# A linear-attention and expert kernel: the state's recurrence issued step by step, and the bonus of two units computed as a matrix product

## The chip, the cores and the metric

The kernel runs on one core of a Trainium2 chip (trn2). The time of a kernel is the device time in microseconds of one execution. A run of the profiler gives, for one execution, the start and the duration of each instruction on the engines: PE (TensorE, matrix products; PEld is its weight load), DVE (VectorE), ACT (ScalarE), POOL (GpSimd), and SP, which issues the DMAs. Engines run side by side, each through its own list of instructions in the order of the program; they wait for each other through semaphores.

## What is computed

The reference has two parts. The first is a recurrence over 768 tokens for 4 batches and 8 heads of width 48; the second is a set of 4 causal attention experts over its output, of which each token uses two.

```python
for t in range(S):                       # S = 768, D = 48
    cur = einsum('bhd,bhe->bhde', u * kt, vt)
    y[:, :, t] = einsum('bhd,bhde->bhe', rt, state + cur)
    state = wt[..., None] * state + einsum('bhd,bhe->bhde', kt, vt)
...
x = y.transpose(0, 2, 1, 3).reshape(B, S, H * D)
logits = x @ w_gate                      # the two largest of 4 experts, softmax over them
for e in range(E):                       # Hd = 64
    a = softmax(causal(x @ wq[e] @ (x @ wk[e]).T / 8))
    out += weight(e) * (a @ (x @ wv[e]) @ wo[e])
```

The term with `u` is called the bonus below: for a token it adds v, times the sum over d of r·u·k, to that token's own row and to no other.

## The kernel before

**Tiling.** The recurrence is cut into chunks of 64 tokens, so that a chunk's work is matrix products and only a 48 x 48 state per head goes from chunk to chunk. A unit is 384 tokens (6 chunks, 3 tiles of 128) of one batch; there are 8 units, and in each 4 pairs of heads. Names in the profile carry the unit and the pair: `ups4_20` belongs to unit 4, pair 2 (the last digit tells which of two banks). Units 0, 2, 4, 6 begin a batch, and 1, 3, 5, 7 go on with its state.

**One pair** (function `one`, L368 on). Two DMAs bring `lt` (decays w, then k, then r, with the head's dimension on the partitions: 391 + 384 + 384 columns) and `nat` (v, k and r, each 288 columns, with tokens on the partitions). DVE runs two scans over the decays, backwards into `suf` (L410) and, from the reciprocal of the chunk's product (L412), forwards into `pre` (L414). Then, on DVE or POOL as the planner decides: `kt` = k·suf (L417) and r·pre into `pre` (L419, called mr by the planner). The bonus is three operations: `nat`'s k times u (L423, uk), times r (L425, ur), and a sum over each head's 48 columns on DVE into `rk` (L428); ACT (L435) or DVE or POOL (L437) puts `rk` on the diagonal of `am` (dg). PE transposes `kt` (L447, then a copy to `kts`), makes the products inside a chunk (`aps`, L459), which DVE copies into `am` under a mask (L465), and the keys times values of each chunk (`ups`, L478, two banks of PSUM). The state's recurrence is L484: for each of the 6 chunks (5 in units 1, 3, 5 and 7, whose last state nobody needs) one DVE instruction of 112 x 48, new state = decay x old state + `ups`, each needing the one before. They are one entry of the plan, a function called `chain`, so they stand one behind the other. A state of each chunk, scaled by the decay (`ys`, L492), is what PE multiplies into `yb` (L513, for two pairs at once); `yi` (L526) is the chunk's own part from `am` and v. Their sum `xi` (L536) is split into a high and a low part, `xx` (L545 on ACT and L547; pair 3 goes to `xs` and from there through six small DMAs, L559, into the free rows of `xx`).

**One group** of the experts (function `moe`, L574 on) takes a unit's `xx`: projections of queries and keys (`pp`, L611), of values and gate logits (`vp`, L634), scores (`sp`, L702), a maximum on DVE (L708), the exponential on ACT (L714), transposes (`tp`, L727), the weighted values (`yp`, L758), the gates, and the output projection (`op`, L830). The last unit is two groups, 7 and 8.

**What sets the order.** Everything is recorded as entries with a cost per engine, and a planner (`Plan.order`, L128 on) puts them one after the other by due times, costs and the waits between engines that it assumes; the engine for an entry is chosen there too. Due times are shifted by tables of numbers per kind (`OFF`, `OFF0` for unit 0, `OFFE` per engine, `SH` per unit or group). What the planner leaves is the fixed list of each engine. Where it expects PE to wait for over a microsecond in the first 60, it adds matmuls without a use (L900), and 14 of them stand at the start (L874). PSUM's eight banks and the buffers of SBUF (`lt` has 3, for example) are planned in the same way: an entry cannot stand before its buffer is free. The chain is recorded so:

```python
plan.add("ss", {"DVE": 118 * nh}, chain, [suf, ku + (k % 2, 0)] + ups,
         [ku + (k % 2, 1)] + ([] if last else [ku + (1 - k % 2, 0)]))
```

Before anything else DVE builds masks (L290 to L319), and the weights of the experts are split into a high and a low part (L332 on ACT, L334 on DVE or POOL).

## Time and profile before

| what | us |
| --- | --- |
| median of 3 runs (lowest, highest) | 370.32 (367.99, 371.35) |
| the profiled execution, its own time | 371.82 |
| its span, first to last instruction | 370.0 |
| PE, DVE, ACT, POOL busy in the span | 335.5, 323.3, 223.8, 183.6 |

The mean clock that PE was granted is 0.962 of full speed. In lines of groups, `xcount | busy, mean ns | idle` is the number of instructions, their busy time in us with the mean duration of one in ns, and how long their engine stood idle before them, with what ended most of that. In a timeline the first column is the start in us and the second the time until the last of the merged instructions ends. A merged group's instructions overlap where the next one starts before the last has ended, so the starts tell the rate.

### The profile page before, as it was taken

What the parts mean: (1) busy time and instruction counts of PE and PEld (TensorE: products, weight loads), DVE (VectorE), ACT (ScalarE), POOL (GpSimd) and SP (SyncE); (2) the same over time, 40 slices, a digit from 0 to 9 for tenths busy, and PEclk for the clock granted to TensorE, in tenths of its full rate; (3) what the DMA queues carried; (4) which work ended last, traced back from release to release, by engine and by line L of the source; (5) the groups of instructions that cost most, each with busy time, mean ns of one, the idle gap of its engine ahead of it and who ended that gap; (6) DMA issues with size and microseconds to landing.
All of it is one profiled execution on the core that took longest, in us unless ns stands there. A gap on an engine that the chain in (4) does not pass through costs nothing.

```text
span 370.0 us, 12837 instructions
## 1 busy us (share of the span) xinstructions
PE 335.5 (91%) x5030; PEld 277.0 (75%) x5030; DVE 323.3 (87%) x989; ACT 223.8 (60%) x663; POOL 183.6 (50%) x311
## 2 busy tenths in 40 slices
PE   8847699689998998989899999889999999999996
PEld 3424469668887797889688697879787888898975
DVE  8997999879998899998999999998899988855871
ACT  2173344387576687474578692775587764854873
POOL 3524455464693383775556643773745743402120
PEclk9895999799997899999999999999999999999999
DMA  7835174252260355522322835352345201210101
GB/s 287 322 89 167 50 212 170 66 169 46 102 204 26 115 192 160 178 78 89 111 78 106 232 96 162 97 145 81 95 161 178 57 8 47 61 39 0 66 2 64
DMA packets 15470, 42.63 MB, mean 115 GB/s; under 512 B 2225, under 2 KB 6834, under 8 KB 15410
## 3 DMA queue, kind: packets, MB, share of 16 engines
q1 hardware_dynamic: 15410, 41.81, 35.8%
q8 instruction: 40, 0.66, 0.7%
q14 instruction: 20, 0.16, 0.2%
HBM read 34.73 MB, written 4.72 MB: 107 GB/s over the span
## 4 chain that ended last, share of the span: by engine, by line
PE 52%; DVE 35%; issue 5%; ACT 3%; DMA 3%; POOL 1%; SPq 0%; DVEq 0%; POOLq 0%; ACTq 0%
PE pp L611 10%; DVE ss L484 9%; PE tp L727 8%; PE op L830 6%; PE yp L758 6%; PE sp L702 6%; PE vp L634 5%; DVE pre L414 4%; DVE a L708 3%; DVE suf L410 3%; PE yi L526 3%; PE yb L513 2%; DVE xi L536 2%; DMA xx<-xs 2%; DVE pre L419 2%
## 5 line engine op out<-in xcount | busy, mean ns | idle before, releaser
L714 ACT ACTIVATE a<-a,mx 128x128 f32<-128x128 f32 (+5 forms) x96 | 63.8, 667 | 13.2 <-DVE mx L708 12.8
L435 ACT ACTIVATE am<-ident,rk 128x64 f32<-128x64 f32 x168 | 43.1, 337 | 23.4 <-DVE rk L428 23.4
L611 PE MATMUL pp<-xx,wh_qk 128*128 128x384 f32 (+2 forms) x216 | 56.5, 329 | 0.2 <-DMA xx<-xs 0.2
L727 PE MATMUL tp<-ident,a 128*128 128x128 f32 x336 | 48.1, 284 | 2.2 <-DVE ss L484 1.7
L484 DVE SCALAR_TENSOR_TENSOR ss<-ss,suf,ups 112x48 f32<-112x48 f32 x160 | 41.9, 263 | 7.8 <-PE ups L478 0.7
L708 DVE CUSTOM_DVE_ANT_0 a<-sp,cmask 128x384 f32<-128x384 f32 (+4 forms) x96 | 43.5, 496 | 2.3 <-PE sp L702 1.4
L419 POOL TENSOR_TENSOR pre<-lt,pre 128x384 f32<-128x384 f32 x24 | 23.7, 988 | 43.2 <-DVE pre L414 37.3
L727 PEld LDWEIGHTS tp<-ident,a 128*128 128x128 f32 x336 | 38.9, 145 | 6.8 <-ACT ATa L243 1.3
L611 PEld LDWEIGHTS pp<-xx,wh_qk 128*128 128x128 f32 x216 | 38.7, 188 | 1.3 <-DVE mx L708 0.5
L758 PE MATMUL yp<-ATa,v_sb 128*64 128x384 f32 (+2 forms) x256 | 36.5, 413 | 1.6 <-DVE ss L484 1.4
L423 POOL TENSOR_TENSOR nat<-nat,u_sb 128x288 f32<-128x288 f32 x28 | 27.8, 996 | 15.3 <-ACT u_sb L243 8.8
L611 PE MATMUL pp<-xx,wl_qk 128*128 128x384 f32 (+2 forms) x108 | 35.0, 324 | 0.0
L243 ACT COPY ATa<-tp 128x512 f32<-128x512 f32 (+3 forms) x69 | 30.6, 479 | 6.3 <-PE tp L727 5.9
L414 DVE TENSOR_TENSOR_SCAN pre<-lt,inv_pre 128x390 f32<-128x390 f32 x32 | 33.8, 1056 | 0.0
L417 POOL TENSOR_TENSOR kt<-lt,suf 128x384 f32<-128x384 f32 x28 | 29.7, 1062 | 8.1 <-DVE suf L410 4.9
L410 DVE TENSOR_TENSOR_SCAN suf<-lt,one_suf 128x390 f32<-128x390 f32 x32 | 32.7, 1033 | 0.5 <-DMA lt<-in_wkr_dram 0.5
L634 PE MATMUL vp<-wh_vg,xx 128*128 128x260 f32 x144 | 30.8, 294 | 0.4 <-DVE ss L484 0.2
L702 PE MATMUL sp<-Kh,Qh 64*128 64x384 f32 (+4 forms) x128 | 26.6, 368 | 4.2 <-DVE ss L484 4.2
L758 PEld LDWEIGHTS yp<-ATa,v_sb 128*64 128x64 f32 x256 | 18.1, 136 | 15.6 <-issue 8.0
L459 PE MATMUL aps<-pre,kt 64*64 64x64 f32 x768 | 20.0, 230 | 9.6 <-DVE am L465 3.5
L545 ACT CAST xx<-xi 112x384 fp32r<-112x384 f32 x24 | 12.2, 510 | 24.0 <-DVE xi L536 23.0
L459 PEld LDWEIGHTS aps<-pre,kt 64*64 64x64 f32 x768 | 16.2, 139 | 13.6 <-issue 5.8
(353 smaller groups left out, 862.4 us busy)
## 6 DMA issues: line engine op xcount, KB each, us to landing
lt<-in_wkr_dram SPq DMA_DIRECT2D x32, 579.5 KB, 4.8
nat<-in_nat_dram SPq DMA_DIRECT2D x32, 432.0 KB, 3.9
...
uf<-in_uN_dram SPq DMA_DIRECT2D x1, 1.5 KB
```

The costliest lines, as they stand in the source:

```text
L410: plan.add("suf", {"DVE": t_scan(wb)}, lambda e: nc.vector.tensor_tensor_scan(rev(suf(), wb), rev(w_(), wb), rev(one_suf, wb), 0.0, op0=AL ...
L414: plan.add("pre", {"DVE": t_scan(wb)}, lambda e: nc.vector.tensor_tensor_scan(pre()[:, 0:wb - 1], w_()[:, 0:wb - 1], flat(inv_pre[:, 0:nh] ...
L435: nc.scalar.mul(am()[:, h, i], ident2, rk()[:, i, h:h + 1])
L459: nc.tensor.matmul(aps[h]()[half(q), i * C:(i + 1) * C], kt()[half(h), c, :], pv()[half(h), c, 0:C], start=True, stop=True)
L484: nc.vector.scalar_tensor_tensor(sv(c + 1), zero[0:112] if c == s0 == 0 else sv(c), sfv()[0:112, c, 0:1], ups[c % 2]()[0:112, c // 2 * D:( ...
L611: nc.tensor.matmul(pp()[:, 0:W], w[:, qk, k, cs], xx()[:, x, k, x0:x0 + W], start=(k == j == 0), stop=(k == j == 2))
L634: nc.tensor.matmul(vp()[:, 0:260], xx()[:, x, k, o], w[:, k, :], start=(k == j == 0), stop=(k == j == 2))
L702: nc.tensor.matmul(sps[x]()[:, 0:w], q()[p, t], k()[p, o], start=j == 0, stop=j == 2)
L708: plan.add("max", {"DVE": t_dve(w) + T_RED}, lambda e, x=x, a=a, mx=mx, h=h, o=o, m=m, sps=sps: nc.vector.tensor_tensor_reduce(a()[:, o], ...
L714: plan.add("exp", {"ACT": t_exp(n)}, lambda e, x=x, y=y, mx=mx, a=a: nc.scalar.activation(a()[:, 0:n], a()[:, 0:n], AF.Exp, bias=mx[-1](), ...
L727: nc.tensor.transpose(tp()[:, j * 128:(j + 1) * 128], a()[:, (j0 + j) * 128:(j0 + j + 1) * 128], ident)
L758: nc.tensor.matmul(yp()[e * 64:e * 64 + 64, lo:W], v_sb[ep]()[:, j, e * 64:e * 64 + 64], at, start=(j == 0), stop=(j == nj - 1))
```

## The change

Three edits and new numbers.

**The chain in single steps.** The function `chain` is gone; each of the 6 instructions is an entry of its own, with a cost of `t_dve(D)` (65 + 1.042 x 48 = 115 in the planner's units, instead of 118 as a sixth of the whole). Each step waits for the one before through a key of its own, and a table `LAG` adds 60 to the time at which the planner lets a step's result be used. Other DVE entries may now stand between two steps. `ys` waits for all steps that it reads.

**The bonus of units 0 and 1.** For these (`k < BON`, with `BON = 2`) k·r is formed from `lt` (kr, on DVE or POOL; it overwrites the first 384 columns of `lt`, the decays, which both scans have read), PE multiplies each tile of 128 tokens by a small table `u2` with u of both heads (rp, three matmuls of 128 x 2 per pair, in a bank of PSUM), and DVE or ACT copies the result to `rk`. uk, ur and the sum L428 are left out there, and the `nat` load of these units is 304 columns (v and 16 more) instead of 864. `u2` is a new input (128 x 8), laid out on the host from u, with its own DMA. The first `lt` load is cut into two, decays first.

**Planned anew.** The tables of due times, `SLACK`, `LEAD`, `MV`, `STAY`, `T0` and `T1` have new values, so the whole order differs. In numbers of instructions: PE has 24 rp matmuls, and 31 in place of 57 matmuls without a use. DVE gets 7 of the 8 kr, 14 instead of 8 of mr, 6 instead of 2 of ur, none instead of 4 of uk, 24 instead of 32 sums, 15 instead of 12 `ys`, 12 instead of 9 of the split of the experts' result (`yl`), and one instead of three of the weight splits. POOL has 18 of mr instead of 24, 24 of uk instead of 28, 18 of ur instead of 30, one kr and three weight splits instead of one. ACT has the other 7 copies of `rk`.

The core of the diff, with the number tables cut to the kinds spoken of:

```diff
-BOTH = {"DVE": {"dg", "ys", "xl", "suf", "pre", "kt", "mr", "uk", "ur", "ux", "yl", "wsplit", "carry", "gate", "masks"},
-        "POOL": {"ys", "kt", "mr", "uk", "ur", "dg", "xl", "yl", "gate", "g4", "wsplit"}}
+BOTH = {"DVE": {"dg", "kr", "ys", "xl", "suf", "pre", "kt", "mr", "uk", "ur", "ux", "yl", "wsplit", "carry", "gate", "masks"},
+        "POOL": {"ys", "kr", "kt", "mr", "uk", "ur", "dg", "xl", "yl", "gate", "g4", "wsplit"}}
...
-                x["ready"][e] = max(x["ready"].get(e, 0.0), end)
+                x["ready"][e] = max(x["ready"].get(e, 0.0), end + LAG.get(o["kind"], 0.0))
...
-def rwkv_moe(ctx: ExitStack, tc: tile.TileContext, wkr, nat, uN,
+def rwkv_moe(ctx: ExitStack, tc: tile.TileContext, wkr, nat, uN, uT,
...
+    u2 = cst.tile([128, 2 * NP], F32, name="u2")
...
-            load("ld", lambda: lt()[:, 0:lw], wkru[p], lw, [(lt, 0), (lt, 1)], first)
+            if turn == 0 and first:
+                load("ld", lambda: lt()[:, 0:wb], wkru[p][:, 0:wb], wb, [(lt, 0)], first)
+                load("ld", lambda: lt()[:, wb:lw], wkru[p][:, wb:lw], lw - wb, [(lt, 1)], first)
+            else:
+                load("ld", lambda: lt()[:, 0:lw], wkru[p], lw, [(lt, 0), (lt, 1)], first)
...
-            load("ldn", lambda: na()[:, 0:9 * nt * 32], natu[p], 9 * nt * 32, [(na, a) for a in range(3)], first)
+            cn = nt * 96 + 16 if k < BON else nt * 288
+            load("ldn", lambda: na()[:, 0:cn], natu[p][:, 0:cn], cn, [(na, a) for a in range(3)], first)
...
-            plan.add("uk", prod(nt * 96), lambda e: E_[e].tensor_tensor(
-                third(1), third(1), u_sb[:, None, p * 96:(p + 1) * 96].to_broadcast([128, nt, 96]), op=ALU.mult), [(na, 1), "u"], [(na, 1)])
-            plan.add("ur", prod(nt * 96), lambda e: E_[e].tensor_tensor(third(2), third(2), third(1), op=ALU.mult),
-                     [(na, 1), (na, 2)], [(na, 2)])
...
-            plan.add("rk", {"DVE": t_dve(nt * 96)}, lambda e: nc.vector.tensor_reduce(
-                rk()[:, 0:nt], third(2).rearrange("p i (h d) -> p i h d", h=2), axis=AX.X, op=ALU.add), [(na, 2)], [rk])
+            if k < BON:
+                plan.add("kr", prod(nh * C), lambda e: E_[e].tensor_tensor(
+                    lt()[:, 0:nh * C], lt()[:, wb:wb + nh * C], lt()[:, wb + nh * C:wb + 2 * nh * C], op=ALU.mult), [(lt, 1)], [(lt, 0)])
+                rp = bank("mo", f"rp{n}")
+
+                def bonus(e):
+                    for i in range(nt):
+                        nc.tensor.matmul(rp()[:, 2 * i:2 * i + 2], lt()[0:112, i * 128:(i + 1) * 128], u2[0:112, 2 * p:2 * p + 2],
+                                         start=True, stop=True)
+                plan.add("rp", {"PE": 110 * nt}, bonus, [(lt, 0), "u2"], [rp])
+                plan.add("rk", {"DVE": 75, "ACT": 60}, lambda e: copy(e, rk()[:, 0:nt].rearrange("p i h -> p (i h)"), rp()[:, 0:2 * nt]), [rp], [rk])
+            else:
+                plan.add("uk", prod(nt * 96), lambda e: E_[e].tensor_tensor(
+                    third(1), third(1), u_sb[:, None, p * 96:(p + 1) * 96].to_broadcast([128, nt, 96]), op=ALU.mult), [(na, 1), "u"], [(na, 1)])
+                plan.add("ur", prod(nt * 96), lambda e: E_[e].tensor_tensor(third(2), third(2), third(1), op=ALU.mult),
+                         [(na, 1), (na, 2)], [(na, 2)])
+                plan.add("rk", {"DVE": t_dve(nt * 96)}, lambda e: nc.vector.tensor_reduce(
+                    rk()[:, 0:nt], third(2).rearrange("p i (h d) -> p i h d", h=2), axis=AX.X, op=ALU.add), [(na, 2)], [rk])
...
-            plan.add("dg", dict(prod(nh * C), ACT=225 * nh), diag, [rk, kt, pre], [am])
+            plan.add("dg", dict(prod(nh * C), ACT=240 * nh), diag, [rk, kt, pre], [am])
...
-            def chain(e):
-                for c in range(nh - (1 if last else 0)):
-                    nc.vector.scalar_tensor_tensor(sv(c + 1), zero[0:112] if c == s0 == 0 else sv(c), sfv()[0:112, c, 0:1],
-                                                   ups[c % 2]()[0:112, c // 2 * D:(c // 2 + 1) * D], op0=ALU.mult, op1=ALU.add)
-            plan.add("ss", {"DVE": 118 * nh}, chain, [suf, ku + (k % 2, 0)] + ups, [ku + (k % 2, 1)] + ([] if last else [ku + (1 - k % 2, 0)]))
+            def key(c):
+                return ku + ((k + c // nh) % 2, c % nh)
+
+            def step(e, c):
+                nc.vector.scalar_tensor_tensor(sv(c + 1), zero[0:112] if c == s0 == 0 else sv(c), sfv()[0:112, c, 0:1],
+                                               ups[c % 2]()[0:112, c // 2 * D:(c // 2 + 1) * D], op0=ALU.mult, op1=ALU.add)
+            for c in range(nh - (1 if last else 0)):
+                plan.add("ss", {"DVE": t_dve(D)}, lambda e, c=c: step(e, c), [suf, ups[c % 2], key(c)], [key(c + 1)])
...
-            plan.add("ys", prod((nh - f) * D), scaled, [suf, ku + (k % 2, 0), ku + (k % 2, 1)], [ky] + ([ky + (0,)] if f == 0 else []))
+            plan.add("ys", prod((nh - f) * D), scaled, [suf] + [key(c) for c in range(f, nh)], [ky] + ([ky + (0,)] if f == 0 else []))
...
+    plan.add("ldu2", {"SP": 475}, lambda e: nc.sync.dma_start(u2, uT), [], ["u2"])
...
-FLEX, LATE, SLACK = (True, True, 64.3)
+FLEX, LATE, SLACK = (True, True, 86.5)
...
-OFF = {'ups': -624.57, 'ys': -258.27, 'ss': -74.21}
+OFF = {'ups': -1164.5, 'ys': 3.08, 'ss': -195.79, 'kr': 181.13, 'rp': 18.51}
...
+LAG = dict(ss=60)
+BON = 2
...
-    arrs = dict(wkr=np.concatenate(wkr), nat=np.concatenate(nat), uN=u.reshape(1, DM), wqk=wqk, wvg=wvg, wo=wo_)
+    uT = np.zeros((2, 64, NP, 2), f)
+    for h in range(2):
+        uT[h, 0:D, :, h] = u.reshape(NP, 2, D)[:, h].T
+    uT = uT.reshape(128, 2 * NP)
+    arrs = dict(wkr=np.concatenate(wkr), nat=np.concatenate(nat), uN=u.reshape(1, DM), uT=uT, wqk=wqk, wvg=wvg, wo=wo_)
```

Three places in the order follow. Rows are instructions as they stand, line numbers are those of each kernel's own file (so the state's step is L484 before and L504 in the change), and `DVE` names its rows with the tile that is written, an arrow, and the tiles read.

On DVE, the chain of unit 4, pair 2, before:

```order
L484 SCALAR_TENSOR_TENSOR ss0_80<-zero_82,suf4_2_2573,ups4_20_3261 112x48
L484 SCALAR_TENSOR_TENSOR ss0_80<-ss0_80,suf4_2_2573,ups4_21_3264 112x48
L484 SCALAR_TENSOR_TENSOR ss0_80<-ss0_80,suf4_2_2573,ups4_20_3261 112x48
L484 SCALAR_TENSOR_TENSOR ss0_80<-ss0_80,suf4_2_2573,ups4_21_3264 112x48
L484 SCALAR_TENSOR_TENSOR ss0_80<-ss0_80,suf4_2_2573,ups4_20_3261 112x48
L484 SCALAR_TENSOR_TENSOR ss1_81<-ss0_80,suf4_2_2573,ups4_21_3264 112x48
L465 COPY_PREDICATED am4_2_3207<-dec_mask_96,aps4_20_3275 128x192
L465 COPY_PREDICATED am4_2_3207<-dec_mask_96,aps4_21_3278 128x192
```

and in the change:

```order
L504 SCALAR_TENSOR_TENSOR ss0_80<-zero_82,suf4_2_2646,ups4_20_3237 112x48
L483 COPY_PREDICATED am4_2_3134<-dec_mask_97,aps4_20_3253 128x192
L483 COPY_PREDICATED am4_2_3134<-dec_mask_97,aps4_21_3256 128x192
L504 SCALAR_TENSOR_TENSOR ss0_80<-ss0_80,suf4_2_2646,ups4_21_3240 112x48
L245 COPY xi4_1_3323<-yb4_1_3271 112x384
L504 SCALAR_TENSOR_TENSOR ss0_80<-ss0_80,suf4_2_2646,ups4_20_3237 112x48
L557 TENSOR_TENSOR xi4_0_3320<-yi4_00_3304,xi4_0_3320 112x3x64
L557 TENSOR_TENSOR xi4_0_3320<-yi4_01_3307,xi4_0_3320 112x3x64
L504 SCALAR_TENSOR_TENSOR ss0_80<-ss0_80,suf4_2_2646,ups4_21_3240 112x48
L557 TENSOR_TENSOR xi4_1_3323<-yi4_10_3325,xi4_1_3323 112x3x64
L557 TENSOR_TENSOR xi4_1_3323<-yi4_11_3328,xi4_1_3323 112x3x64
L504 SCALAR_TENSOR_TENSOR ss0_80<-ss0_80,suf4_2_2646,ups4_20_3237 112x48
```

The six steps stood one behind the other, and the masked copies of the pair after them. Now the masked copies and the additions of `xi` of pairs 0 and 1 stand between the steps, and only the last two steps follow each other directly.

On DVE, the start of unit 0, from the first step of pair 0, before:

```order
L484 SCALAR_TENSOR_TENSOR ss0_80<-zero_82,suf0_0_143,ups0_00_170 112x48
L484 SCALAR_TENSOR_TENSOR ss0_80<-ss0_80,suf0_0_143,ups0_01_179 112x48
L484 SCALAR_TENSOR_TENSOR ss0_80<-ss0_80,suf0_0_143,ups0_00_170 112x48
L484 SCALAR_TENSOR_TENSOR ss0_80<-ss0_80,suf0_0_143,ups0_01_179 112x48
L484 SCALAR_TENSOR_TENSOR ss0_80<-ss0_80,suf0_0_143,ups0_00_170 112x48
L484 SCALAR_TENSOR_TENSOR ss1_81<-ss0_80,suf0_0_143,ups0_01_179 112x48
L414 SCALAR_TENSOR_TENSOR pre0_1_219<-lt0_1_122,inv_pre_69 128x390
L492 TENSOR_TENSOR ys0_85<-ss0_80,suf0_0_143 112x240
L419 TENSOR_TENSOR pre0_1_219<-lt0_1_122,pre0_1_219 128x6x64
L410 SCALAR_TENSOR_TENSOR suf0_2_233<-lt0_2_153,one_suf_66 128x390
L412 RECIPROCAL inv_pre_69<-suf0_2_233 128x6
L423 TENSOR_TENSOR nat0_0_139<-nat0_0_139,u_sb_84 128x288
```

and in the change:

```order
L504 SCALAR_TENSOR_TENSOR ss0_80<-zero_82,suf0_0_141,ups0_00_219 112x48
L420 SCALAR_TENSOR_TENSOR pre0_2_276<-lt0_2_143,inv_pre_69 128x390
L423 TENSOR_TENSOR kt0_2_278<-lt0_2_143,suf0_2_198 128x384
L425 TENSOR_TENSOR pre0_2_276<-lt0_2_143,pre0_2_276 128x6x64
L431 TENSOR_TENSOR lt0_2_143<-lt0_2_143 128x384
L483 COPY_PREDICATED am0_0_237<-dec_mask_97,aps0_00_172 128x192
L483 COPY_PREDICATED am0_0_237<-dec_mask_97,aps0_01_176 128x192
L504 SCALAR_TENSOR_TENSOR ss0_80<-ss0_80,suf0_0_141,ups0_01_222 112x48
L504 SCALAR_TENSOR_TENSOR ss0_80<-zero_82,suf0_1_187,ups0_10_244 112x48
L504 SCALAR_TENSOR_TENSOR ss0_80<-ss0_80,suf0_0_141,ups0_00_219 112x48
L504 SCALAR_TENSOR_TENSOR ss0_80<-ss0_80,suf0_1_187,ups0_11_247 112x48
L504 SCALAR_TENSOR_TENSOR ss0_80<-ss0_80,suf0_0_141,ups0_01_222 112x48
```

The chain of pair 0 and its `ys` stood ahead of the work on pair 2. Now the forward scan, `kt`, mr and kr of pair 2 (L420 to L431) and the masked copies of pair 0 stand behind its first step, its other steps alternate with those of pair 1, and its `ys` follows 16 rows behind the first step instead of 7. The `nat` product with u (L423 before) is no longer there.

On PE, the end of the value projection of group 6 before, where unit 7's last `yb` and `yi` follow it:

```order
L634 MATMUL vp6_2_5798<-wh_vg_115,xx6_4932 128x260 x2
L634 MATMUL vp6_2_5798<-wl_vg_116,xx6_4932 128x260
L634 MATMUL vp6_2_5798<-wh_vg_115,xx6_4932 128x260 x2
L634 MATMUL vp6_2_5798<-wl_vg_116,xx6_4932 128x260
L634 MATMUL vp6_2_5798<-wh_vg_115,xx6_4932 128x260
L513 MATMUL yb7_2_5817<-pre7_2_5507,ys2_89 64x64
L513 MATMUL yb7_3_5819<-pre7_3_5540,ys3_91 48x64
L513 MATMUL yb7_2_5817<-pre7_2_5507,ys2_89 48x64
```

and its beginning in the change, where all `yi` of unit 7 stand ahead of it:

```order
L723 MATMUL sp6_1000_5858<-Kl31_5688,Qh6_1_5633 128x128
L723 MATMUL sp6_1010_5860<-Kl31_5688,Qh6_1_5633 128x128
L723 MATMUL sp6_1000_5858<-Kh31_5664,Ql6_1_5646 128x128
L723 MATMUL sp6_1010_5860<-Kh31_5664,Ql6_1_5646 128x128
L655 MATMUL vp6_0_5873<-wh_vg_116,xx6_4847 128x260
L655 MATMUL vp6_0_5873<-wl_vg_117,xx6_4847 128x260
L655 MATMUL vp6_0_5873<-wh_vg_116,xx6_4847 128x260 x2
L655 MATMUL vp6_0_5873<-wl_vg_117,xx6_4847 128x260
L655 MATMUL vp6_0_5873<-wh_vg_116,xx6_4847 128x260
```

Before, the 27 matmuls of `vp6` stood ahead of the last `yb` of unit 7; now the 27 stand behind the last `yi` of unit 7, among the scores and transposes of group 6. The 6 `gb` matmuls and the `gp` transpose of group 5 have gone the same way.

16 lines of the change are left out of this document (8 added, 8 removed).

## The prediction, made before the changed kernel ran

> **What bounds the kernel now.** I read the page first: busy shares, then the chain that ended last by engine.
>
> ```profile
> PE 335.5 (91%) x5030; PEld 277.0 (75%) x5030; DVE 323.3 (87%) x989; ACT 223.8 (60%) x663; POOL 183.6 (50%) x311
> PE 52%; DVE 35%; issue 5%; ACT 3%; DMA 3%; POOL 1%; SPq 0%; DVEq 0%; POOLq 0%; ACTq 0%
> ```
>
> PE and DVE share the chain, so neither is the bound everywhere. A view of windows splits the span where the kinds of work change: the first low part of a query (`Ql`, L618) at 61.6, and 315.5, after the last addition of `xi`. The columns are the window's length, then busy time (and count) of PE, PEld, DVE, ACT and POOL. The fourth line is the same view for PE's matmuls without a use (L900) alone, and the last three are the chain of waits by line inside 0 to 62, 62 to 315 and 315 to 370 (the program cuts these lines at their end).
>
> ```profile
> 0.00:61.60 61.60, 48.01 (x692) 30.24 (x693) 56.45 (x126) 22.25 (x62) 29.88 (x46) 0.89 0.55 186
> 61.60:315.50 253.90, 236.43 (x3892) 202.33 (x3892) 233.33 (x738) 165.99 (x497) 143.46 (x224) 0.97 0.37 114
> 315.50:370.00 54.50, 51.02 (x452) 44.44 (x450) 33.50 (x128) 35.61 (x105) 10.24 (x41) 0.99 0.12 39
> 0.00:61.60 61.60, 16.10 (x57) 5.60 (x57) 0.89 0.55 186
> by line: DVE pre L414 12.6%; DVE pre L419 10.0%; DVE ss L484 9.9%; DVE suf L410 9.6%; issue 7.9%; PE yb L900 4.3%; DVE am L465 3.5%; DVE xx L547 3.2%; DVE dec_mask L291 3.0%; PE yb L513 2.7%; DVE kt L417 2.5%; DVE rk L428 2.5%; DVE ys L492
> by line: PE pp L611 11.3%; DVE ss L484 10.0%; PE tp L727 8.0%; PE sp L702 5.9%; PE vp L634 5.2%; PE op L830 5.2%; PE yp L758 5.1%; issue 5.0%; DVE a L708 4.6%; DVE pre L414 3.4%; PE yi L526 3.4%; DVE xi L536 2.8%; PE yb L513 2.7%; DMA xx<-x
> by line: PE yp L758 19.1%; PE op L830 18.5%; PE tp L727 17.3%; PE sp L702 15.6%; PE pp L611 15.1%; PE vp L634 6.4%; PE gb L803 1.2%; ACT ob L243 0.9%; PE gp__6685 L792 0.3%; PE gp__6622 L792 0.3%; PE gp__6155 L792 0.1%; issue 0.1%; ACTq L24
> ```
>
> Three stages, then. The start is DVE's: 56.5 of 61.6 us busy, nearly every line of its chain is DVE, and a third of PE's 48 is L900. The middle is both: 236 and 233 of 254, with the chain going back and forth; the state's step alone is 10% of it, some 25 us. The end is PE's (51 of 54.5), and the recurrence has nothing left there. So I work the sum out by stage: DVE's work for the first two, PE's for the third.
>
> **The step.** The timeline of DVE around one chain (unit 4, pair 2):
>
> ```profile
> 159.77 0.26 DVE L484 SCALAR_TENSOR_TENSOR ss<-zero,suf,ups 112x48 f32<-112x48 f32 x1
> 160.06 1.46 DVE L484 SCALAR_TENSOR_TENSOR ss<-ss,suf,ups 112x48 f32<-112x48 f32 x5
> 161.44 0.28 DVE L708 CUSTOM_DVE_ANT_0 a<-sp,cmask 128x128 f32<-128x128 f32 x1
> L484 DVE SCALAR_TENSOR_TENSOR ss<-ss,suf,ups 112x48 f32<-112x48 f32 x160 | 41.9, 263 | 7.8 <-PE ups L478 0.7
> ```
>
> Five steps take 1.46 us and one lasts 0.263, so they start (1.46 - 0.263)/4 = 0.299 us apart: each waits for the one before to end, and 0.036 more. The last starts at 160.06 + 4 x 0.299 = 161.26 and ends at 161.52, but the maximum behind it, which needs nothing of it, starts at 161.44. A step that nobody waits for thus holds the engine for 0.185 us, 0.08 less than it lasts. What the change can win per step is 0.299 - 0.185 = 0.114 us, if something of at least that length stands between. Of the 176 steps 32 begin a chain; of the other 144, 23 still follow their forerunner directly in the change's order (as the last two of the place shown), which leaves 121 x 0.114 = 13.8 us.
>
> The Trainium skill speaks against this: VectorE: DVE Perf Modes, in "The DRAIN you can't avoid" and "Rules for kernel authors", says that the next operation does not start before the pipe is empty, that a semaphore costs nothing on top, and that one should reduce the count of operations rather than their waits. By it the saving would be nothing; the row that starts at 161.44, 0.08 us before the step ahead of it ends, disagrees with it.
>
> **What else moves on DVE.** The rows that price it, DVE first and then POOL:
>
> ```profile
> L428 DVE TENSOR_REDUCE rk<-nat 128x6 f32<-128x288 f32 x32 | 14.0, 437 | 0.0
> L419 DVE TENSOR_TENSOR pre<-lt,pre 128x384 f32<-128x384 f32 x8 | 8.0, 999 | 0.0
> L417 DVE TENSOR_TENSOR kt<-lt,suf 128x384 f32<-128x384 f32 x4 | 2.2, 544 | 0.0
> L423 DVE TENSOR_TENSOR nat<-nat,u_sb 128x288 f32<-128x288 f32 x4 | 2.1, 520 | 1.4 <-DMA nat<-in_nat_dram 1.4
> L425 DVE TENSOR_TENSOR nat<-nat 128x288 f32<-128x288 f32 x2 | 1.4, 716 | 0.0
> L334 DVE TENSOR_TENSOR wl_vg<-w_vg,wh_vg 128x780 fp32r<-128x780 f32 x1 | 0.9, 940 | 0.0
> L334 DVE TENSOR_TENSOR wl_qk<-w_qk,wh_qk 128x768 fp32r<-128x768 f32 x1 | 0.9, 933 | 0.0
> L492 DVE TENSOR_TENSOR ys<-ss,suf 112x240 f32<-112x240 f32 x6 | 2.4, 394 | 0.0
> L536 DVE TENSOR_TENSOR xi<-yi,xi 112x192 f32<-112x192 f32 x64 | 19.1, 346 | 2.7 <-PE yi L526 1.5 <-ACT a L714 1.0 <-ACT xi L243 0.3
> 9.10 0.53 DVE L419 TENSOR_TENSOR pre<-lt,pre 128x384 f32<-128x384 f32 x1
> 25.59 2.17 DVE L419 TENSOR_TENSOR pre<-lt,pre 128x384 f32<-128x384 f32 x1
> L423 POOL TENSOR_TENSOR nat<-nat,u_sb 128x288 f32<-128x288 f32 x28 | 27.8, 996 | 15.3 <-ACT u_sb L243 8.8 <-DMA nat<-in_nat_dram 6.3
> L425 POOL TENSOR_TENSOR nat<-nat 128x288 f32<-128x288 f32 x30 | 25.4, 848 | 1.0
> L419 POOL TENSOR_TENSOR pre<-lt,pre 128x384 f32<-128x384 f32 x24 | 23.7, 988 | 43.2 <-DVE pre L414 37.3 <-DVE m__4749 L658 4.9 <-DVE gg__2381 L776 0.9
> L334 POOL TENSOR_TENSOR wl_qk<-w_qk,wh_qk 128x768 fp32r<-128x768 f32 x1 | 2.1, 2052 | 6.9 <-ACT wh_qk L332 6.9
> ```
>
> One product on DVE (L419) is 0.53 us in one place and 2.17 in another, a mean of 1.0: these are slowed by something beside them. I bound them by 0.53 and the mean.
>
> Start (rows of DVE's order up to the first `Ql`). Gone: 6 sums at 0.44 (2.6), one uk and one ur (1.2), two weight splits (1.9), one mr (1.0): 6.7. New: 7 kr, priced as the like-sized `kt` at 0.54 (3.8), 5 more steps at 0.185 (0.9), two `ys` (0.8) and two halves of `xi` (0.7): 6.2. Spread steps: 25 x 0.114 = 2.9. Together **-3.4**.
>
> Middle. Spread steps: 96 x 0.114 = 10.9, and 5 steps fewer, 0.9. Gone: two sums, three uk (2.4). New: 7 mr (7.0, or 3.7 undisturbed), 5 ur (3.6, or 2.2). Copies and small things cancel to within 2. Together between -4 and -9; I take **-8**, near the upper end, because POOL, whose work disturbs DVE, loses 4 uk, 12 ur and 6 mr and gets two splits and little else, about 16 us less by its rows.
>
> **PE at the end.** The timeline before the last `yi`; from the third row to the fourth there are 15 matmuls of `vp`, 0.126 us apart:
>
> ```profile
> 310.34 0.36 PE L634 MATMUL vp<-wh_vg,xx 128*128 128x260 f32 x1 [0.21 <-DVE ss L484]
> 310.91 0.49 PE L803 MATMUL gb<-gT__5768,sel 128*128 128x128 bf16 x6
> 311.21 0.36 PE L634 MATMUL vp<-wh_vg,xx 128*128 128x260 f32 x1
> ...
> 312.98 0.28 PE L634 MATMUL vp<-wh_vg,xx 128*128 128x260 f32 x1
> 313.20 0.93 PE L513 MATMUL yb<-pre,ys 48*64 48x64 f32 x48
> ```
>
> Group 6's `vp` filled PE while DVE finished unit 7. In the change its 27 matmuls stand behind the last `yi`: 27 x 0.126 = 3.4, and the 6 `gb` 0.3, in a stage where PE is busy 94%: **+3.8** with the one `gp`. That is a price of the new order, paid where nothing hides it.
>
> **What I cost at nothing.** 24 rp matmuls: 8 sets of three; a set of `ktp` (three 128x128) is the nearest row, 0.52 us, so at most 4.2. They fall in the start, where PE still has matmuls without a use to drop (57 become 31); uncovered they'd be those 4.2. The 7 copies of `rk` go to ACT, which is busy 22 of 61.6 there. Behind the first rp on PE's list stand the `ups` of pairs 0 and 1, so a late kr or `u2` would hold the first steps too; rp stands behind the `ktp` of pair 1, whose `kt` comes later on DVE than the first kr, and that is its cover. DMA: 8 `nat` loads shrink by 560 columns, 2.3 MB; yet the first scan starts behind a mask, not behind its load, and the split of that load wins nothing as long as the masks take that long:
>
> ```profile
> 7.37 0.52 PE L447 MATMUL ktp<-ident,kt 128*128 128x128 f32 x3
> 5.59 0.17 DVE L319 TENSOR_SCALAR tri<-tri 128x16 f32<-128x16 f32 x1
> 5.66 0.96 DVE L410 TENSOR_TENSOR_SCAN suf<-lt,one_suf 128x390 f32<-128x390 f32 x1
> lt<-in_wkr_dram SPq DMA_DIRECT2D x32, 579.5 KB, 4.8
> ```
>
> New is that an `lt` buffer of units 0 and 1 comes free only after PE's rp, so SP's queue of loads waits for PE. The load of unit 1's pair 3 waits for kr and rp of its pair 0, and the scan that needs it stands 22 rows of DVE behind that kr, about 8 us by the durations of such rows before, against 4.8 to land. Without that cover the scans of pairs 2 and 3 would each be late by up to 4.8.
>
> **Sum.** -3.4 - 8 + 3.8 = -7.6 against the profiled span of 370.0: 362.4. That execution took 371.82 in all, 1.8 more than its span, and lay 1.5 over the median of 370.32, so the median to expect is 362.4 + 1.8 - 1.5 = **362.7**. Its own range is 357 to 368: the middle at -4 gives 367, at -9 and a start better by 4 gives 358.
>
> **Rivals.** (a) More than the sum. The old plan counted a chain of 6 at 6 x 118 = 708 units of its time, the trace shows 5 x 0.299 + 0.26 = 1.76 us, so all behind each of 32 chains stood about 1 us too early in the plan. The new plan holds 115 + 60 for the next step, closer. If that also ends half of the 20.6 us that DVE idles in the middle (253.9 - 233.3), it is 10 us more: 353. Against it: the idle time is in pieces under 1.3 us, answers of other engines. Chance 0.15.
>
> (b) PE is the bound in the middle. 236 of 253.9 is as high as DVE's share, and half the chain is PE; then the 8 us show up as more idle DVE, and 362.7 + 8 = 370.7 remains. For it speaks the chain's first line (PE pp); against it, that PE's busy time there counts matmuls that stood waiting on DVE, as the 0.21 above. 0.19.
>
> (c) Slower: the spread chain ends late. What is behind it waits already:
>
> ```profile
> POOL ys L492 <- DVE ss L484: 27.3, 19, 3.2
> ACT am L435 <- DVE rk L428: 23.4, 14, 6.2
> ```
>
> `ys` needs the last states, `yb` needs `ys`, and on PE's list everything behind `yb` stands still. Adding DVE's rows from a chain's first to its last step gives 1.7 us before, and on average 3.6 in the change (12 for unit 0's pair 2, whose steps lie 27 rows apart). 1.9 us in each of 8 units, with nothing on PE to fill, is 15: 378. It decides from the point where PE reaches `yb` before DVE has passed the last step. 0.13.
>
> (d) Slower: the step's pace does not depend on who follows, so spreading saves nothing: 13.8 back, 376.5. The row at 161.44 is against it. 0.03. It is also what the Trainium skill's page named above would give here.
>
> **How the numbers follow.** My forecast has 0.50. A measurement of this kernel tells about 1% from no change, so faster means under 366.6: nearly all of mine (0.47) and (a), 0.62. Same takes most of (b) and the rest of mine, 0.21; slower is (c), (d) and a little of (b), 0.17. The range of 351 to 372 holds (a), mine and (b) and leaves (c) and (d) out.
>
> **What would show it.** Steps between other rows with a pitch near 0.185, and DVE's busy time for them plus their idle time down by over 10 us; the first `Ql` near 58, the last `xi` near 304, the end 58 long. Wrong would be: PE waits for `ss` or `ys` that grow past their present few us (c), a middle as long as before with DVE idle by 28 us (b), or a chain share of `ss` still near 10% (d).

## The result, and the profile after

The changed kernel takes **352.49 us** (median of 4 runs, 350.69 to 355.21) against 369.15 for the kernel before, a ratio of 0.955 with a 95% interval of 0.946 to 0.964. The forecast was 362.7 with a range of 351 to 372: direction and range hold, but 16.7 us came off where the sum had 7.6, and the result lies outside the sum's own 357 to 368. The profiled execution took 355.21 us, the longest of the four, with a span of 353.4.

The first two lines are the page's busy shares and its chain by engine; then come the three stages by windows, cut at the first `Ql` (57.8) and the last addition into `xi` (295.9), with the same columns as before.

```profile
PE 329.7 (93%) x5049; PEld 274.2 (78%) x5052; DVE 311.5 (88%) x1001; ACT 223.3 (63%) x666; POOL 170.1 (48%) x288
PE 70%; DVE 20%; ACT 4%; issue 2%; POOL 1%; DMA 1%; POOLq 0%; ACTq 0%; DVEq 0%
```

```profile
0.00:57.80 57.80, 45.57 (x744) 31.75 (x748) 49.92 (x130) 24.05 (x70) 21.10 (x36) 0.76 0.48 156
57.80:295.90 238.10, 230.06 (x3829) 195.04 (x3829) 225.62 (x735) 163.74 (x491) 137.81 (x210) 0.99 0.39 123
295.90:353.40 57.50, 54.10 (x482) 47.46 (x478) 35.92 (x138) 35.47 (x108) 11.16 (x42) 1.00 0.12 37
```

| stage | before | after | moved | forecast |
|---|---|---|---|---|
| start | 61.6 | 57.8 | -3.8 | -3.4 |
| middle | 253.9 | 238.1 | **-15.8** | **-8** |
| end | 54.5 | 57.5 | +3.0 | +3.8 |

Start and end came as worked out. The whole miss is in the middle. There VectorE's busy time fell from 233.3 to 225.6 (-7.7), and its idle time from 20.6 to 12.5 (-8.1). Of the idle time, 5.6 us are the steps' own: a step that reads an earlier state stood idle behind the one ahead for 6.4 us in sum before and 0.9 after. All other waits of VectorE fell by 2.5. The chain of waits by line, for the start and then the middle:

```profile
by line: PE rp L437 7.6%; DMA nat<-in_nat_dram 6.3%; DVE pre L420 6.3%; DVE suf L416 6.1%; DVE lt L431 6.0%; PE yb L534 6.0%; issue 4.3%; PE ktp L922 4.2%; PE pp L632 4.1%; PE ktp L465 4.0%; PE ups L496 3.9%; PE yi L547 3.6%; DVE pre L425 3
by line: PE pp L632 15.9%; PE tp L748 10.2%; PE vp L655 9.0%; PE sp L723 7.8%; PE yp L779 6.9%; PE op L851 6.5%; DVE ss L504 4.0%; PE yi L547 3.7%; PE yb L534 3.1%; DVE pre L420 3.1%; PE ups L496 3.0%; PE ktp L465 2.7%; PE aps L477 2.6%; DV
```

In the middle the state's step went from 10.0% of the chain to 4.0%, and PE's lines moved up into its place: `pp` 11.3 to 15.9, `vp` 5.2 to 9.0. In the start a new line leads, the `rp` matmuls (7.6% of 57.8 us is 4.4 us), which I had costed at nothing.

VectorE around one chain (unit 4, pair 2), and the group of the steps:

```profile
176.29 0.26 DVE L504 SCALAR_TENSOR_TENSOR ss<-zero,suf,ups 112x48 f32<-112x48 f32 x1
176.46 0.64 DVE L483 COPY_PREDICATED am<-dec_mask,aps 128x192 f32<-128x192 uint32 x2
176.99 0.26 DVE L504 SCALAR_TENSOR_TENSOR ss<-ss,suf,ups 112x48 f32<-112x48 f32 x1
177.16 0.55 DVE L245 COPY xi<-yb 112x384 f32<-112x384 f32 x1
...
179.04 0.56 DVE L504 SCALAR_TENSOR_TENSOR ss<-ss,suf,ups 112x48 f32<-112x48 f32 x2
```

```profile
L504 DVE SCALAR_TENSOR_TENSOR ss<-ss,suf,ups 112x48 f32<-112x48 f32 x160 | 37.4, 256 | 1.8 <-PE ups L496 0.5
```

A parted step lasts 0.26 us and the next instruction starts 0.17 behind its start (176.29 to 176.46, 176.99 to 177.16). The two that still stand together at 179.04 take 0.56 for both, so 0.56 - 0.26 = 0.30 apart, as in the old block. Busy and idle time of this group went from 41.9 + 7.8 to 37.4 + 1.8, which is 10.5 us less. The busy time counts a step in full even where the next instruction starts before its end, so the time that the steps hold VectorE fell by more (worked out below).

### The profile page after: what moved, and what is told of

Its sections match the earlier page's. It is cut to its first block, busy times and chain, and to the rows that moved or that the text cites. A ratio compares the mean times of both kernels' runs of the same rounds, so it can differ in the third digit from the quotient of the medians.

```text
span 353.4 us, 12854 instructions
## 1 busy us (share of the span) xinstructions
PE 329.7 (93%) x5049; PEld 274.2 (78%) x5052; DVE 311.5 (88%) x1001; ACT 223.3 (63%) x666; POOL 170.1 (48%) x288
## 4 chain that ended last, share of the span: by engine, by line
PE 70%; DVE 20%; ACT 4%; issue 2%; POOL 1%; DMA 1%; POOLq 0%; ACTq 0%; DVEq 0%
PE pp L632 14%; PE tp L748 10%; PE vp L655 8%; PE yp L779 7%; PE sp L723 7%; PE op L851 7%; DVE ss L504 3%; DVE pre L420 3%; PE yb L534 3%; PE yi L547 3%; PE ups L496 3%; PE ktp L465 3%; PE aps L477 2%; DVE suf L416 2%; DVE xi L557 2%
## 5 line engine op out<-in xcount | busy, mean ns | idle before, releaser
L504 DVE SCALAR_TENSOR_TENSOR ss<-ss,suf,ups 112x48 f32<-112x48 f32 x160 | 37.4, 256 | 1.8 <-PE ups L496 0.5
L420 DVE TENSOR_TENSOR_SCAN pre<-lt,inv_pre 128x390 f32<-128x390 f32 x32 | 36.0, 1124 | 0.1
L423 POOL TENSOR_TENSOR kt<-lt,suf 128x384 f32<-128x384 f32 x28 | 30.2, 1084 | 9.7 <-PE aps L477 7.3
L655 PE MATMUL vp<-wh_vg,xx 128*128 128x260 f32 x144 | 33.1, 310 | 0.2 <-DVE am L483 0.2
L243 ACT COPY ATa<-tp 128x512 f32<-128x512 f32 (+3 forms) x62 | 28.2, 481 | 7.9 <-PE tp L748 7.6
L568 POOL TENSOR_TENSOR xx<-xi,xx 112x384 fp32r<-112x384 f32 x15 | 16.8, 1125 | 30.4 <-ACT xx L566 30.2
L416 DVE TENSOR_TENSOR_SCAN suf<-lt,one_suf 128x390 f32<-128x390 f32 x32 | 30.9, 965 | 0.5 <-DMA lt<-in_wkr_dram 0.5
L425 POOL TENSOR_TENSOR pre<-lt,pre 128x384 f32<-128x384 f32 x18 | 16.9, 936 | 26.8 <-DVE pre L420 25.8
L243 ACT COPY kts<-ktp 128x384 f32<-128x384 f32 x29 | 13.7, 480 | 22.0 <-PE ktp L465 22.0
L442 POOL TENSOR_TENSOR nat<-nat,u_sb 128x288 f32<-128x288 f32 x24 | 24.2, 1009 | 7.0 <-DMA nat<-in_nat_dram 2.9
L779 PEld LDWEIGHTS yp<-ATa,v_sb 128*64 128x64 f32 x256 | 16.4, 136 | 13.7 <-issue 10.5
L655 PEld LDWEIGHTS vp<-wh_vg,xx 128*128 128x128 f32 x144 | 25.6, 203 | 0.5 <-DVE am L483 0.4
## 6 DMA issues: line engine op xcount, KB each, us to landing
out_dram<-ob SPq DMA_DIRECT2D x24, 192.0 KB, 1.9
```

The costliest lines, as they stand in the source:

```text
L243: nc.scalar.copy(o, i)
L416: plan.add("suf", {"DVE": t_scan(wb)}, lambda e: nc.vector.tensor_tensor_scan(rev(suf(), wb), rev(w_(), wb), rev(one_suf, wb), 0.0, op0=AL ...
L420: plan.add("pre", {"DVE": t_scan(wb)}, lambda e: nc.vector.tensor_tensor_scan(pre()[:, 0:wb - 1], w_()[:, 0:wb - 1], flat(inv_pre[:, 0:nh] ...
L504: nc.vector.scalar_tensor_tensor(sv(c + 1), zero[0:112] if c == s0 == 0 else sv(c), sfv()[0:112, c, 0:1], ups[c % 2]()[0:112, c // 2 * D:( ...
L655: nc.tensor.matmul(vp()[:, 0:260], xx()[:, x, k, o], w[:, k, :], start=(k == j == 0), stop=(k == j == 2))
L779: nc.tensor.matmul(yp()[e * 64:e * 64 + 64, lo:W], v_sb[ep]()[:, j, e * 64:e * 64 + 64], at, start=(j == 0), stop=(j == nj - 1))
```

## The experiments

Three theories at first: **A**, half of the gain is the step's shorter hold on VectorE, half the new order; **B**, the steps are everything; **C**, the order is everything. After the first runs they gave way to **U**: what VectorE takes and the plan does not know is what lengthens the run.

### The same order, other steps

**e1**: the changed order with each chain in one block again.

```diff
+        if o["kind"] == "ss":
+            for x in plan.ops[o["n"] + 1:]:
+                if x["kind"] != "ss" or not x["deps"] <= gone:
+                    break
+                x["fn"]("DVE")
+                gone.add(x["n"])
```

> The changed kernel with its own order of everything else; only the six steps of a chain are issued in one piece again, at the place of the first of them. All 144 dependent steps then stand directly behind the one before (23 in the changed kernel). Theory A (half and half: the shorter pitch of the steps is worth what the sum says, 121 x 0.114 us = 13.8 us of VectorE time of which some 8 to 11 us lie on the path, and the rest of the gain is the new order's): 8 to 11 us slower than the changed kernel, 361 to 364 us. Theory B (the steps are everything: the idle time of VectorE went only because a chain no longer holds VectorE for 1.76 us at a time): 13 to 17 us slower, 366 to 370 us. Theory C (the new order is everything, the steps' pitch is hidden): at most 3 us slower, 353 to 356 us.

Measured: 380.03 us (ratio to before 1.029, 1.023 to 1.035), 27.5 slower than the changed kernel and 11 slower than the kernel before. More than any theory had. The middle:

```profile
63.80:321.00 257.20, 233.17 (x3832) 196.43 (x3833) 237.00 (x734) 164.77 (x492) 136.66 (x210) 0.99 0.36 113
```

VectorE's busy time there is up 11.4 us (225.6 to 237.0), but the stage is 19.1 longer; over the whole span it is up 16.7 (311.5 to 328.2). C falls. B is nearest, and short by 10.

**e5**: is it the block that hurts, or the time? The changed order, its steps parted, with a small addition that nobody reads ahead of each dependent step.

```diff
             def step(e, c):
+                if c > 0:
+                    nc.vector.tensor_tensor(junk[c % 4][0:112], zero[0:112], zero[0:112], op=ALU.add)
```

> The changed kernel in its own order, single steps parted as they are, but ahead of each of the 144 dependent steps VectorE adds two 112x48 tiles into a tile that nobody reads (a 128x48 sum took 0.12 us from one start to the next in the profile of before). Where a step stood directly behind the one before (23 times) this fills the time in which it waited; 121 times it adds about 0.116 us: 14.0 us of VectorE time, as much as the shorter pitch had saved, but in pieces of 0.116 us and not in blocks of 1.76 us. Theory H (what costs is that a block holds VectorE; e1 lost 27 us by that): 10 to 15 us slower than the changed kernel, 362 to 368 us. Theory V (VectorE's time counts however it is spent, and about as much idle time of VectorE comes with it, as in e1): 20 to 27 us slower, 372 to 380 us. Theory C (the pitch is hidden): at most 4 us slower.

Measured: 386.04 us (1.048, 1.038 to 1.057), 33.5 slower than the changed kernel.

```profile
63.10:326.30 263.20, 236.42 (x3819) 196.65 (x3820) 252.97 (x847) 163.31 (x485) 133.73 (x209) 0.97 0.35 110
L506 DVE TENSOR_TENSOR junk<-zero 112x48 f32<-112x48 f32 x144 | 53.4, 371 | 0.0
```

VectorE is busy 253 of 263 us. The additions took far more than the 14.0 us for which H and V were priced: counted from the end of the instruction ahead to their own, 110 of them took 0.12 us each, as expected, but the other 34 took 28.1 us together, one of them over 5. VectorE's busy time over the whole span rose by 35.4 us (311.5 to 346.9). So the run grew by about what was put on VectorE, 33.5 for 35.4, which is the rate of H and not the doubling of V; this run does not tell against H. In e1 it was 27.5 for 16.7. Time that is put on VectorE against the plan lengthens the run, in pieces (0.9 for one) and in blocks (1.6 for one).

**e2**: the kernel before, its order on each engine untouched, with the steps spread among the VectorE instructions that follow.

```diff
+        if o["e"] == "DVE":
+            for x in list(left):
+                step1(x)          # one step of each chain that has begun
+        if o["kind"] == "ss":
+            left.append(o)
+            step1(o)
```

> The kernel before, each engine's order as it was, but the six steps of a chain stand one by one behind the VectorE instructions that follow them (two or more in a row only where something on VectorE needs the end of the chain). 66 of 144 dependent steps still stand directly behind the one before, 78 are parted. Nothing is planned anew and the bonus is as before. 78 x 0.114 us = 8.9 us less VectorE time. Theory A: 5 to 8 us faster than before, 361 to 364 us. Theory B: 9 to 12 us faster, 357 to 360 us. Theory C: no faster, 367 to 374 us, since ys and the products after it only come later.

Measured: 403.24 us (1.092, 1.087 to 1.098), 34 us slower than before. All three theories miss. Its waits for the steps, and its middle:

```profile
POOL ys L493 <- DVE ss L484: 55.6, 20, 6.8
PE sp L703 <- DVE ss L484: 11.9, 7, 2.6
PE aps L459 <- DVE ss L484: 7.1, 4, 2.6
```

```profile
60.40:348.00 287.60, 249.20 (x3899) 211.55 (x3899) 232.51 (x740) 168.22 (x497) 141.36 (x224) 0.92 0.32 101
```

This is rival (c) of the prediction in the flesh: VectorE has less to do, but the chains end late, `ys` waits 55.6 us for them instead of 27.3, and PE, which stands behind, waits too. Spreading without a plan that knows of it is a loss.

**e6 and e7**: less work on VectorE, with no step touched, in the old and in the new order. Left out is the second of the two additions into `xi`, so half of the within-chunk part is missing in the output.

```diff
-                    for q in range(2):
+                    for q in range(1):
                         x = xi()...
```

> The kernel before in its own order, chain in one piece; left out is the second of the two additions into xi (half of the within-chunk part is missing in the output): 32 VectorE instructions at 0.265 us from start to start, 8.5 us of VectorE time less, nothing else. Theory V (idle time goes with the busy time): 13 to 18 us faster than before, 351 to 356 us. Theory A (VectorE's time counts one for one in the start and the middle): 7 to 9 us faster, 360 to 363 us. Theory F (the order of before is fitted to its times, and whatever VectorE saves is lost in waits): at most 4 us faster, 365 to 370 us.

> The changed kernel with the same 32 additions left out, 8.5 us of VectorE time less. In its middle PE is busy 230.1 of 238.1 us, so there is at most 8 us to gain there unless PE itself gets faster. Theory V: 4 to 8 us faster than the changed kernel, 344 to 349 us. Theory P (PE bounds the middle now): at most 4 us faster, 348 to 353 us.

Measured: e6 371.46 us (0.997, 0.992 to 1.003), e7 352.39 (0.951, 0.942 to 0.961). VectorE's busy time over the span fell by 8.6 us in e6 and by 5.8 in e7, and neither gains anything that can be told from the spread of its runs (365.92 to 374.75 and 349.00 to 356.59). The middle of e6:

```profile
61.20:314.80 253.60, 237.05 (x3891) 203.18 (x3891) 227.71 (x713) 166.17 (x497) 142.80 (x224) 0.96 0.37 114
```

VectorE is busy 227.7 instead of 233.3 and the stage is as long as before; the saved time is idle time now. A and V fall for this part of VectorE's work; F (e6) and P (e7) named the right times. So a microsecond of VectorE has no fixed price: one more than the plan cost 0.9 to 1.6 in e5 and e1, and one less is worth nothing here. Why the additions in particular buy nothing in the order of before, where VectorE runs late anyhow, these two runs do not say.

### Planned anew with the tables as they are

**e3**: the kernel before with the changed kernel's tables. **e4**: the changed kernel with the old bonus (`BON = 0`). **e8** was meant to put the old bonus into the changed order; but the size of the rows that are loaded is a cost in the plan, so it was planned anew too, against what its expectation says.

```diff
-BON = 2
+BON = 0
```

> The kernel before (chain as one entry, bonus as before) planned with the tables of the changed kernel: due times, shifts, slack. Theory A: the tables belong to the costs that the plan holds for single steps, and bring little of the order's half alone: 363 to 372 us. Theory B: no gain, 367 to 376 us. Theory C (the tables are what found the time): 352 to 358 us.

> The changed kernel with BON = 0: single steps and the new tables, but the bonus of every unit by uk, ur and rk as in the kernel before, planned anew with that. Theories A, B and C alike: within 3 us of the changed kernel, 350 to 356 us, since the first two units' bonus was costed at little. Theory D (the extra 8 us come from the bonus: ACT's wait for the rk sums fell from 23.4 to 2.2 us, POOL is relieved): 6 to 9 us slower than the changed kernel, 358 to 362 us.

> The changed kernel with its own order of everything else; only the bonus of the first two units is as before: k*u and the product with r on POOL at the place of the rp matmuls (16 instructions of 0.92 us on POOL), the sum over d on VectorE (8 of 0.36 us from start to start, against 8 products kr, most of them on VectorE, that go) at the place of the masks' diagonal, and k and r loaded in rows again. Nothing is planned anew. Theory D (the extra 8 us are the bonus's): 6 to 12 us slower than the changed kernel, 358 to 365 us. Theories A and V (the bonus is worth little): at most 4 us slower, 352 to 357 us.

Measured: e3 383.43 us (1.042, 1.033 to 1.050), e4 371.50 (1.005, 1.001 to 1.008), e8 370.46 (1.001, 0.997 to 1.006). e3 is slower than any theory had. e4 and e8 are 18 to 19 us slower than the changed kernel, twice what theory D asked for. But so small an edit moves the whole order: the plan's own end, a number that the code works out while the kernel is built, and no time of the chip, is 328.8 us in the changed kernel, 349.8 in e4 and 342.3 in e8. These runs tell that a table of due times belongs to one program, and not what the bonus is worth. C falls again with e3.

### Planned anew, with tables searched for each program

The plan's end set against the profiled span gave theory U: before, 326.8 against 370.0; changed, 328.8 against 353.4. Both plans also give the middle the same length, 226.5 and 225.2 us. The chip took 253.9 and 238.1. So I searched the tables' numbers anew for each program (small random moves, kept where the plan's end came earlier), with a price of the chain that is true to the trace (e9, e10, e11) and, as a control, with the old one (e12).

```diff
 e9   (kernel before)   {"DVE": 118 * nh}   ->  {"DVE": 299 * nh}
 e10  (changed kernel)  {"DVE": t_dve(D)}   ->  {"DVE": 185}, LAG = dict(ss=-13)
 e11  as e10, BON = 0
 e12  (kernel before)   tables alone
```

> The kernel before, chain still in one piece and bonus as before, but the plan holds 299 units for a step instead of 118 (its units are ns; the trace showed 0.299 us), and the numbers of its tables (due times, shifts, slack, stay) are searched anew for that price, by the end that the plan reckons: 342.4 us, against 326.8 for the kernel before, whose plan left out 32 x (1.76 - 0.71) = 33.7 us of chains. Theory U (what VectorE takes and the plan does not know is what lengthens the run: the profiled spans are 43.2 us over the plan's end in before, 24.6 in the changed kernel, and steps that the plan does not know make 33.7 of the one and 121 x 0.07 + 23 x 0.184 = 12.7 of the other, which leaves 9.5 and 11.9): 342.4 + 9.5 to 12 + 1.8, so 353 to 357 us. Theory S (the gain is the step's shorter hold on VectorE itself; a block stays a block): 363 us or more.

> The changed kernel, but the plan holds 185 units for a step and 299 from one step of a chain to the next (115 and 302 in the changed kernel), with the numbers of its tables searched anew for that; the plan's end is 329.6 us, 328.8 in the changed kernel. Theory U: nothing of the steps is left out any more, so 329.6 + 9.5 to 12 + 1.8: 341 to 344 us, some 9 us faster than the changed kernel. Theory P (PE, busy 230.1 of 238.1 us in the middle of the changed kernel, is the bound now): at most 3 us faster, 349 to 354 us.

> A control for the search: the kernel before with its own price of a chain (118 units a step) and the numbers of its tables searched anew in the same way; the plan's end moves from 326.8 to 324.4 us. Theory U: the chains are still left out, so about 2.4 us faster than before at most, 365 to 371 us. Theory T (searching the tables again is what wins): 360 us or less.

> Single steps priced true (185 and 299 units, as in e10), but the bonus of every unit by uk, ur and rk as in the kernel before (as in e9), the tables' numbers searched anew for that; the plan's end is 332.0 us. It stands between e9 (block, old bonus: 354.2 us measured, plan's end 342.4) and e10 (single steps, new bonus: 346.8 measured, plan's end 329.6). Theory U: the measured times were 11.8 and 17.1 us over the plan's end in e9 and e10, so 344 to 349 us; the single steps are then worth 5 to 10 us beside e9 and the bonus at most 3. Theory D (the bonus by TensorE carries what e10 won over e9): 352 to 356 us. Theory S (the step's shorter hold carries it, and the plan's reckoning does not tell): 346 to 348 us, so that it could not be told from Theory U here.

Measured:

| kernel | chain | bonus | us | ratio to before |
|---|---|---|---|---|
| e12 | block, 118 a step | old | 363.06 | 0.984 (0.979 to 0.989) |
| e9 | block, 299 a step | old | 354.23 | 0.962 (0.958 to 0.965) |
| changed | steps, 115 and 302 | new | 352.49 | 0.955 (0.946 to 0.964) |
| e11 | steps, 185 and 299 | old | 350.44 | 0.950 (0.946 to 0.955) |
| e10 | steps, 185 and 299 | new | **346.76** | 0.942 (0.938 to 0.945) |

e9 is the run that decides. Its chains are the old blocks, and yet it stands level with the changed kernel. U's range is met (353 to 357 forecast), S falls. The group of its steps is as in the kernel before (41.9 busy, 7.8 idle there), and the chain of waits in its middle has changed. The second fence has the same two rows of the control, e12:

```profile
L484 DVE SCALAR_TENSOR_TENSOR ss<-ss,suf,ups 112x48 f32<-112x48 f32 x160 | 42.0, 264 | 7.5 <-PE ups L478 0.4
by line: PE pp L611 15.3%; PE yp L758 9.3%; PE tp L727 7.9%; PE vp L634 7.5%; PE op L830 7.4%; PE sp L702 6.3%; DVE a L708 3.9%; PE yb L513 3.6%; DVE ss L484 3.6%; PE aps L459 3.3%; issue 3.0%; PE yi L526 2.9%; PE ups L478 2.9%; PE ktp L447
```

```profile
L484 DVE SCALAR_TENSOR_TENSOR ss<-ss,suf,ups 112x48 f32<-112x48 f32 x160 | 42.0, 264 | 7.5 <-PE ups L478 0.3
by line: DVE ss L484 11.8%; PE pp L611 11.4%; DVE a L708 8.1%; PE tp L727 6.3%; PE vp L634 6.1%; issue 5.9%; PE sp L702 4.3%; PE op L830 3.9%; DVE suf L410 3.2%; DMA nat<-in_nat_dram 2.8%; PE yb L513 2.7%; PE yi L526 2.5%; DVE pre L414 2.5%
```

The same 42.0 us of steps are 11.8% of the chain where the plan thinks a chain takes 0.7 us, and 3.6% where it knows that it takes 1.8. That is not idle time of VectorE which closes. The first two stages of e9, and then of e12:

```profile
0.00:42.98 42.98, 37.41 (x542) 21.26 (x548) 38.97 (x102) 17.90 (x48) 26.82 (x46) 0.96 0.62 214
42.98:296.00 253.02, 238.18 (x4026) 202.84 (x4025) 230.69 (x726) 177.03 (x533) 154.78 (x233) 0.99 0.39 124
```

```profile
0.00:54.34 54.34, 42.98 (x667) 25.82 (x673) 49.21 (x119) 22.29 (x62) 26.81 (x43) 0.91 0.60 203
54.34:308.19 253.85, 235.06 (x3923) 201.66 (x3923) 233.58 (x737) 169.74 (x507) 148.92 (x227) 0.99 0.37 116
```

The first `Ql` comes 11 us earlier in e9, so less of the work lies ahead of the cut, and only the two stages together compare: 296.0 us up to the last `xi` against 308.2. VectorE is busy for 269.7 of them against 282.8, which leaves it idle for 26.3 and 25.4. With the true price in the plan VectorE has 28 instructions fewer there, and POOL (181.6 us against 175.7) and ACT (194.9 against 192.0) are busier; why the rest of VectorE's 13.1 us went, these rows do not tell. The changed kernel compares with the kernel before otherwise: busy 275.5 after 289.8, idle 20.4 after 25.7.

Each new kernel of the table is the outcome of one search. The search alone (e12) is worth 5 to 6 us (1.6%), more than U's 2.4 and less than T asked, the true price 9 more (363.06 to 354.23), single steps beside that 4 (e9 to e11), the bonus by PE 3 to 4 (e11 to e10; the intervals just part). e10 beats both kernels, the changed one by 5.7 us, where U had asked for some 9; e11 too ends a little behind U (344 to 349). The middle of e10 shows why there is little left:

```profile
55.90:289.10 233.20, 229.45 (x3862) 194.56 (x3861) 222.93 (x736) 168.07 (x496) 141.50 (x214) 1.00 0.40 125
```

PE is busy 229.5 of 233.2 us at full clock: 98%. Now PE does bound it, as P said of the changed kernel too early.

All planned kernels, by what the plan holds for a chain of six:

| kernel | the plan holds | plan's end | profiled span | over |
|---|---|---|---|---|
| before, e12, e3 | block of 0.71 us | 326.8, 324.4, 347.7 | 370.0, 362.4, 381.8 | 43.2, 38.0, 34.1 |
| changed, e4, e8 | steps of 0.115, 0.302 apart | 328.8, 349.8, 342.3 | 353.4, 371.5, 368.7 | 24.6, 21.7, 26.4 |
| e9, e10, e11 | the trace's price | 342.4, 329.6, 332.0 | 352.1, 345.0, 344.8 | 9.7, 15.4, 12.8 |

What the plan leaves out is the difference between the time that the steps hold VectorE and the time that the plan holds for them. Before, the steps hold it for 144 x 0.299 + 32 x 0.185 = 49.0 us, of which the plan knew 32 x 0.708 = 22.7; 26.3 were left out (my expectation of e9 said 33.7, as if every chain had six steps; half have five). In the changed kernel the plan has 0.302 from one step to the next where 23 of them follow each other directly, and 0.115 for each of the other 153, which hold VectorE for 0.185: 153 x 0.070 = 10.7 left out, and much the same in e4 and e8. In the last row nothing is. The last column falls in the same steps: 34 to 43, 22 to 26, 10 to 15. With what was left out taken off, it is 16.9, 11.7 and 7.8 in the first row, 13.9, 11.0 and 15.5 in the second, and 9.7, 15.4 and 12.8 in the third, with means of 12 to 13.5. So the time that the plan left out came back about one for one, and what is left scatters over 9 us, from 7.8 to 16.9.

The expectation of e9 had taken 33.7 and 12.7 off, so U's ranges for e9 and e10 were built on too small a rest. With 26.3 and 10.7, which leave 16.9 and 13.9, the same reasoning asks for 358 to 361 us in e9, 345 to 348 in e10 and 348 to 351 in e11. The last two came in there; e9 is 4 us faster, and that it met U's range was luck in part.

## Why the prediction was right in its mechanism and wrong in its size

- **The step, 0.299 to 0.185, 13.8 us on VectorE.** Right, a little low: 0.30 and 0.17 in the trace. For each VectorE instruction of the middle I added the time from the end of the one ahead to its own end: 130 steps that read an earlier state took 39.6 us before (0.304 each), 125 took 24.0 after (0.192). That is -15.6, where the sum had -10.9 - 0.9. The shorter pitch, and five steps fewer at 0.30 instead of 0.185, make up about half of the difference.
- **What else moves on VectorE in the middle.** The sum gave back 3.8 of the steps' 11.8 for new rows there and took -8. By the same reckoning the rest came to -0.2: the new `mr` and `ur` rows are there (+4.4 and +2.0), but `ATb` copies, uk products and waits of the additions into `xi` went (-3.6, -2.6, -2.5). **The middle's term is the one that was mis-sized**: -15.8 instead of -8, outside its bounds of -4 to -9; 3.8 of the missing 7.8 us lie in the steps and 4.0 in the rest, which I had taken to be a cost. That VectorE's busy time fell by 7.7 meets the -8 by accident: the 0.114 a step has 0.036 of idle time in it, and of the 8.1 us of idle time that went, 5.6 are the steps' own.
- **Rival (a)**, that the old plan was wrong by 1 us a chain and that closing the gap ends half of the idle time, was priced 10 us under my sum at a chance of 0.15, and its 353 is the time that was measured. That the plan's error costs time is right: e9 gains 9 us over e12 without any change to the steps. The way is not shown. Apart from the steps' own, VectorE's idle time in the middle fell by 2.5 us where (a) asked for 10, and in e9 its idle time did not fall at all. So that 353 was met is luck in part. How the 16.7 us of the changed kernel divide between the shorter step and the fitted order can't be said: undoing the one inside the other costs more than both together (e1).
- **Rival (b)**: no. PE's busy time in the middle fell with VectorE's (236.4 to 230.1). What I held against it misread the row: the 0.21 is idle time ahead of a matmul and no part of its 0.36. In the changed kernel PE is busy 97% of the middle and e7 gains nothing from less work on VectorE, so PE is close to being the bound there, and in e10 it is.
- **Rival (c)**: not in the changed kernel, where `ys` waits for the steps less than before; e2, which is 34 us slower, shows that it is real, and twice as dear as the 15 us that I had, where no plan knows of the spread.

```profile
POOL ys L513 <- DVE ss L504: 16.2, 10, 3.8
ACT rk L243 <- PE rp L437: 8.0, 4, 4.9
```

- **Rival (d)** falls with the row at 176.46. The rule in the Trainium skill, VectorE: DVE Perf Modes, "The DRAIN you can't avoid", that the next operation waits until the pipe is empty, does not hold here without its exception, which I had left out: the same section adds that a next operation which is not held starts earlier. The rows agree with the exception: an instruction that needs nothing of the step starts 0.09 us before the step has ended, and one that waits for it 0.04 after.
- **The start** was right in sum (-3.8 for -3.4; first `Ql` at 57.8 for 58), with one part costed wrongly: `rp` is on its chain with 4.4 us, about the 4.2 that I had as its bound uncovered, and ACT waits 8.0 us for it (second row above).
- **The end**: +3.0 for +3.8, on PE, as worked out. The last `xi` came at 295.9, 8 us ahead of the 304 forecast, which is the middle's miss again.
